# Attention with adapters: turning queries, keys, last tokens and x by transposing DMA instead of on TensorE, with the adapter's steps in a new order

## The chip, the core and the metric

The kernel runs on one core of one Trainium2 chip, in a single launch. The metric is device time in microseconds, as the median over runs. The profile is one more execution, taken by the hardware profiler. The core's engines work side by side, each through its own list of instructions in order: TensorE (PE, with its weight loads shown as PEld), VectorE (DVE), ScalarE (ACT), GpSimd (POOL), and SyncE (SP), which in this kernel only issues DMAs. Engines wait for each other by semaphores.

## The reference

Two stages follow each other: attention with a relative bias, then a mixture of low-rank adapters on the attention's output.

```python
scores = (1 / np.sqrt(D)) * np.matmul(q, k.transpose(0, 1, 3, 2))    # q, k, v: [8, 8, 576, 64]
bias = bias_table[bucket(abs(i - j))]                                # [576, 576, 8 heads], constant from distance 128 on
attn = softmax(scores + bias.transpose(2, 0, 1)[None])
x = np.matmul(attn, v).transpose(0, 2, 1, 3).reshape(4608, 512)

logits = x @ w_gate                                                  # 8 experts
topk = the two largest logits of each row; w = softmax over these two
delta = sum over the two: w * ((x @ A[e]) @ B[e])                    # A: [8, 512, 16], B: [8, 16, 512]
out = x + delta
```

Inputs and output are float32; the kernel computes products in bfloat16 with float32 sums.

## The kernel before

**Units.** The work is cut into 32 units, one for each of 8 batches (`b`) and 4 pairs of heads (`hp`); `u = 4 b + hp`. Of the 576 tokens of a sequence, the first 512 are treated in four key tiles of 128 (`c`), the last 64 ("last tokens", "tail") apart. The whole order is written out by hand: one loop over `u`, in which each engine's instructions stand in the order in which the engine runs them. Nothing is rearranged later.

**Inputs.** SP loads float32 queries, keys and values of a pair into staging tiles (`load`, L99 to L114), queries and keys four units ahead, values three, and the last tokens of a batch once per batch (`load_tail`). GpSimd casts them to bfloat16 (`cast`, L133 to L143; `cast_tail`), queries and keys two units ahead (`prep`). There are four staging buffers of each kind.

**Turns.** A product on TensorE needs the summed dimension on the partitions, so queries and keys, which arrive with tokens on the partitions, must be turned. `Turn.block` (L298 to L303) does it with four TensorE transposes of 64x64 per 128x128 block. They write into a score tile `tp` in PSUM, and VectorE copies the whole to `qkT` in SBUF (`Turn.copy`, L306). Each unit turns the queries and keys of the next unit: eight blocks (`turn_qk`, `copy_qk`); once per batch also the last tokens' (`turn_tail`, `copy_tail`, into `tls`). The score tiles are three PSUM tiles in rotation: four key tiles, the edges and the turn use them in each unit.

**Scores and exponentials.** `keys` (L346 to L361) makes one key tile's scores of two heads, the product with the queries (L353) and a second one that adds the bias (L358); `keys_exp` (L364) takes the exponential on ScalarE, 128x1024 at a time. `edges` (L386 to L402) makes the products of last tokens with the others, with one exponential per unit (`pt`, L402). `edge_bias` multiplies their bias factors on GpSimd and VectorE. The products among last tokens are made once per batch (`turn_corners`, `corners_exp`, `corners_bias`).

**Values.** One unit later the exponentials are multiplied with the values, which carry a column of ones so that the sum of the softmax comes out too. `values_a` covers query tiles 0 to 2, `values_b` tile 3 and the last tokens (L418, L428, L442). Each writes a PSUM bank of 512 float32 columns. `normalise_a` and `normalise_b` divide by the sum and write x in bfloat16 (`xn`, `xe`, L476 to L489) on VectorE. These banks come from a pool of two (`mm`), which also holds the turned x and the adapters' results.

**Adapters.** A batch's x is complete after four units. Its rows form groups: `g0` and `g1` of two tiles of 128 rows each, and a group of last tokens for two batches together. For each group x is turned on TensorE (`turn_x`, L334) and copied by VectorE (`copy_x`, L338); then come the product with A and the gate (`moe_z` in free columns of a values bank, or `moe_zpair` in a bank of its own), the copy out (`moe_zc`), the choice of two experts (`moe_g`, DVE and POOL), the weights (`moe_w`, ScalarE and POOL), the transpose of the gated z (`moe_t`, L559, copied by `moe_tc`, L562), and the product with B with the sum with x (`moe_d`, L566, L569), after which the group is stored by SP. `moe` enters each step into a table for a later unit; the loop takes the tables' entries at fixed places. For the second to last batch (`early`) the steps follow more closely. Steps that would not be done in time go to `left` and are made after the loop (`late_out`), three tiles in all.

**After the loop** the last batch's x is finished, turned (`last_x` and `turn`) and taken through the same adapter steps with code of its own.

**SP's list** in a unit is: last tokens' load (once per batch), queries and keys of `u + 4`, values of `u + 3`, then the stores where `moe_d` stands. SP takes them in this order; a store whose result is not ready holds what stands behind it.

Of the kernel before, what the change touches and what calls it, by code (L numbers as in the profile page):

```python
# [37 lines left out]
def kernel(  # L38
# [94 lines left out]
    def cast(u, nm, eng):  # L133
        s = stage[(u, nm)].rearrange("p h (c d) -> p h c d", c=4)
        if nm == "v":
            t = vts[u % NV]
            eng.tensor_copy(t[:, :, :, :D].rearrange("p c h d -> p h c d"), s)  # L137
        else:
            t = qkp.tile([128, 4, 2, D], BF16, name=f"{nm}n", tag=f"{nm}n")
            copy = eng.copy if eng is nc.scalar else eng.tensor_copy  # L140
            copy(t.rearrange("p c h d -> p h c d"), s)  # L141
            nat[(u, nm)] = t
# [167 lines left out]
    def turn_qk(t, u):  # L310
        for i, nm in enumerate(("q", "k")):
            n = nat.pop((u, nm))
            for c in range(4):
                t.block(4 * i + c, n[:, c, :, :].rearrange("p h d -> p (h d)"))

    def copy_qk(t, u):
        qkT[u] = qkp.tile([128, 2, SM], BF16, name="qkT", tag="qkT")
        t.copy(qkT[u], 0, 8)

# [9 lines left out]
    def turn_x(gr):  # L329
        n = len(gr.x)  # L330
        gr.xT_ps = mp.tile([128, 2, 4, 128], BF16, name="xT_ps", tag="mm")
        for i, x in enumerate(gr.x):
            for c in range(4):
                nc.tensor.transpose(gr.xT_ps[:, i, c, :], x[:, c * 128:(c + 1) * 128], ident)  # L334

    def copy_x(gr):
        gr.xT = xtp.tile([128, len(gr.x), 4, 128], BF16, name="xT", tag="xT")
        nc.vector.tensor_copy(gr.xT, gr.xT_ps[:, :len(gr.x)])  # L338
# [84 lines left out]
    def pv_last(u, pv, o, t, n=1):  # L423
        b, hp = units[u]
        pt = probs[u][1]
        for h in range(2):
            x0 = 64 + h * SM + 256 + t % 2 * 128
            nc.tensor.matmul(_ap(pv, o + h * W1, [[260, n], [1, W1]]), lhsT=pt[:, x0:x0 + 128],  # L428
# [4 lines left out]
    def pv_tail(u, pv, c, o=130, first=False):  # L433
# [10 lines left out]

    def values_a(u):
        pva[u] = mp.tile([128, 512], FP32, name="pv", tag="mm")
        for t in range(3):
            for c in range(4):
                pv_main(u, pva[u], t * 130, t, c, t == 0 and c == 0)
        pv_last(u, pva[u], 0, 0, 2)  # L450
        pv_last(u, pva[u], 130, 1)
        return pva[u]

    def values_b(u):
        pvb[u] = mp.tile([128, 512], FP32, name="pv", tag="mm")
        for c in range(4):
            pv_main(u, pvb[u], 0, 3, c, c == 0)
        pv_last(u, pvb[u], 0, 3)
        for c in range(5):
            pv_tail(u, pvb[u], c)  # L460
# [11 lines left out]

    def normalise_a(u):
# [3 lines left out]
        nc.vector.tensor_tensor(_ap(xs[b], hp * 128, [[Dm, 3], [D, 2], [1, D]]),  # L477
                                _ap(pv, 0, [[2 * W1, 3], [W1, 2], [1, D]]),
                                _ap(rc, 0, [[2, 3], [1, 2], [0, D]]), op=ALU.mult)

    def normalise_b(u):
# [3 lines left out]
        nc.vector.tensor_tensor(_ap(xs[b], 3 * Dm + hp * 128, [[D, 2], [1, D]]),  # L485
                                _ap(pv, 0, [[W1, 2], [1, D]]),
                                _ap(rc, 6, [[1, 2], [0, D]]), op=ALU.mult)
        rows = slice(64 * (b % 2), 64 * (b % 2) + 64)
        nc.vector.tensor_tensor(xe[b // 2][rows, hp * 128:hp * 128 + 128].rearrange("p (h d) -> p h d", h=2),  # L489
                                _ap(pv[rows], 130, [[W1, 2], [1, D]]), _ap(rc[rows], 8, [[1, 2], [0, D]]),  # L490
                                op=ALU.mult)
# [89 lines left out]
    def group(b, i):  # L581
        gr = Group()
        gr.zT_ps, gr.zT, gr.ot, gr.solo = {}, None, None, False
        if i < 2:
            gr.x = [xs[b][:, c, :] for c in (2 * i, 2 * i + 1)]

# [4 lines left out]
        else:  # L591
            gr.x = [xe[b // 2]]

# [5 lines left out]
    late, second, third, tx, zs, zts, ztb, gate1, after = ({} for _ in range(9))  # L599
# [4 lines left out]
    def moe(b, u):  # L604
        g0, g1 = group(b, 0), group(b, 1)
        tiles = ((g0, 0), (g0, 1), (g1, 0), (g1, 1))
        early = b == B - 2
        at(tx, u + 1 - early, g0)
        at(tx, u + 2 - early, g1)
        if early:  # L610
            for i, g in enumerate((g0, g1)):
                at(late, u + i, moe_zpair, g)
                at(gate1, u + 1 + i, moe_w, g)
# [452 lines left out]
```

## Time and profile before

| | us |
|---|---|
| median of 3 runs | 205.93 |
| the three runs | 204.39, 205.93, 206.39 |
| the profiled execution | 205.11 |
| its span | 203.3 |

| engine | busy us in the span | share |
|---|---|---|
| TensorE | 173.8 | 86% |
| ScalarE | 166.1 | 82% |
| VectorE | 138.3 | 68% |
| GpSimd | 130.9 | 64% |
| DMA engines, SP's queue | | 64.7% of 16 engines |

In the rows quoted below, L353 is line 353 of the kernel, `out<-in` names what an instruction writes and reads, `x32` counts instructions, and sizes are partitions x elements. In the groups, the numbers after the first bar are busy us in all and mean ns of one; those after the second bar are idle time of that engine just before these instructions, with what ended most of it. In a timeline a row begins with its start and its length in us, and a bracket at its end gives the idle time before it. SPq is the queue on which SP issues DMAs.

### The profile page before, as it was taken

What the parts mean: (1) busy time and instruction counts of PE and PEld (TensorE: products, weight loads), DVE (VectorE), ACT (ScalarE), POOL (GpSimd) and SP (SyncE); (2) the same over time, 40 slices, a digit from 0 to 9 for tenths busy, and PEclk for the clock granted to TensorE, in tenths of its full rate; (3) what the DMA queues carried; (4) which work ended last, traced back from release to release, by engine and by line L of the source; (5) the groups of instructions that cost most, each with busy time, mean ns of one, the idle gap of its engine ahead of it and who ended that gap; (6) DMA issues with size and microseconds to landing.
All of it is one profiled execution on the core that took longest, in us unless ns stands there. A gap on an engine that the chain in (4) does not pass through costs nothing.

```text
span 203.3 us, 11419 instructions
## 1 busy us (share of the span) xinstructions
PE 173.8 (86%) x4898; PEld 127.5 (63%) x4898; DVE 138.3 (68%) x411; ACT 166.1 (82%) x205; POOL 130.9 (64%) x321
## 2 busy tenths in 40 slices
PE   0377889899999899989988999999988997999870
PEld 0255666677666677766676677767776685666640
DVE  4314655467667876887877777789877786888750
ACT  3269999998998889989879889889988878788470
POOL 4298546678578647986694947985776577761110
PEclk9999999999999999999999999999999999999999
DMA  5868889679778886855279999862498940042165
GB/s 134 214 192 240 235 243 240 177 212 272 213 208 254 252 218 203 242 173 158 58 196 299 280 242 295 251 203 72 108 280 262 291 167 24 3 157 107 55 241 173
DMA packets 62714, 39.87 MB, mean 196 GB/s; under 512 B 17848, under 2 KB 59336, under 8 KB 62664
## 3 DMA queue, kind: packets, MB, share of 16 engines
q1 hardware_dynamic: 61864, 38.58, 64.7%
q8 instruction: 38, 0.62, 1.3%
q10 hardware_dynamic: 800, 0.56, 1.1%
q14 instruction: 12, 0.10, 0.2%
HBM read 29.67 MB, written 9.46 MB: 192 GB/s over the span
## 4 chain that ended last, share of the span: by engine, by line
PE 51%; ACT 18%; DVE 15%; issue 5%; DMA 5%; POOL 2%; ACTq 0%; POOLq 0%; DVEq 0%
PE pv L418 14%; PE sc L353 10%; ACT pk L364 10%; ACT pt L402 6%; PE sc L358 5%; DVE ot L569 5%; PE xT_ps L334 4%; PE pv L428 3%; PE sc L395 3%; PE tp L302 3%; DVE pt L410 2%; PE sc L400 2%; PE dl L566 2%; PE pv L442 2%; DMA Wt<-g_d 1%
## 5 line engine op out<-in xcount | busy, mean ns | idle before, releaser
L364 ACT ACTIVATE pk<-sc 128x1024 bf16<-128x1024 f32 x128 | 124.1, 1028 | 14.6 <-PE sc L358 13.4
L353 PE MATMUL sc<-qkT 64*64 64x512 bf16 x512 | 52.8, 396 | 3.4 <-ACT pk L364 2.7
L418 PEld LDWEIGHTS <-pk 128*128 128x128 bf16 x1024 | 38.7, 98 | 16.4 <-issue 7.8
L358 PE MATMUL sc<-Wt,anti 64*64 64x384 bf16 (+1 forms) x512 | 44.1, 300 | 1.8 <-DMA Wt<-g_d 1.8
L418 PE MATMUL pv<-v,pk 128*128 128x65 bf16 x992 | 42.7, 194 | 0.9 <-DVE z L522 0.4
L402 ACT ACTIVATE pt<-sc 128x1024 bf16<-128x1024 f32 x32 | 32.8, 1024 | 10.3 <-PE sc L400 5.2
L306 DVE COPY qkT<-tp 128x1024 bf16<-128x1024 bf16 x32 | 22.0, 686 | 6.9 <-PE tp L302 6.2
L410 DVE TENSOR_TENSOR pt<-pt,ET 64x256 bf16<-64x256 bf16 x32 | 15.3, 477 | 15.2 <-ACT pt L402 11.9
L353 PEld LDWEIGHTS <-qkT 64*64 64x64 bf16 x512 | 17.1, 106 | 12.7 <-issue 5.7
L137 POOL CAST v<-vs 128x512 bf16<-128x512 f32 x32 | 20.4, 637 | 6.6 <-DMA vs<-in_v_dram 6.5
L141 POOL CAST kn<-ks 128x512 bf16<-128x512 f32 x31 | 19.4, 626 | 1.1 <-PE sc L358 0.9
L358 PEld LDWEIGHTS <-anti 64*64 64x64 bf16 x512 | 17.9, 108 | 2.9 <-issue 2.9
L569 DVE TENSOR_TENSOR ot<-dl,xn 128x512 f32<-128x512 f32 x25 | 17.3, 691 | 1.3 <-PE dl L566 0.3
L477 DVE TENSOR_TENSOR xn<-pv,rc 128x384 bf16<-128x384 f32 x31 | 17.3, 557 | 1.1
L141 POOL CAST qn<-qs 128x512 bf16<-128x512 f32 x27 | 16.6, 613 | 1.6 <-PE sc L358 0.9
L428 PE MATMUL pv<-vb,pt 128*128 128x65 bf16 (+1 forms) x186 | 17.5, 203 | 0.0
L302 PEld LDWEIGHTS <-qn 64*64 64x64 bf16 x512 | 10.8, 111 | 10.4 <-ACT qn L141 5.3
L532 POOL TENSOR_TENSOR a<-z,top 128x16 f32<-128x16 f32 (+1 forms) x17 | 3.8, 223 | 19.2 <-DVE top L527 19.1
L302 PE MATMUL tp<-ident,qn 64*64 64x64 bf16 x512 | 11.1, 196 | 5.7 <-ACT qn L141 5.3
L562 DVE COPY zT<-pv 128x128 bf16<-128x128 bf16 x31 | 6.7, 221 | 12.0 <-PE pv L559 12.0
L408 POOL TENSOR_TENSOR pt<-pt,ELC 128x128 bf16<-128x128 bf16 x32 | 13.8, 431 | 1.5 <-ACT pt L402 1.4
L442 PE MATMUL pv<-v,pt 128*128 128x65 bf16 x248 | 13.0, 193 | 0.0
(147 smaller groups left out, 337.8 us busy)
## 6 DMA issues: line engine op xcount, KB each, us to landing
qs<-in_q_dram SPq DMA_DIRECT2D x32, 256.0 KB, 3.9
vs<-in_v_dram SPq DMA_DIRECT2D x64, 128.0 KB, 4.0
ks<-in_k_dram SPq DMA_DIRECT2D x62, 128.0 KB, 3.8
out_dram<-ot SPq DMA_DIRECT2D x11, 512.0 KB, 4.2
vt<-in_v_dram SPq DMA_DIRECT2D x8, 128.0 KB, 4.1
out_dram<-fot SPq DMA_DIRECT2D x4, 256.0 KB, 2.4
qkt<-in_q_dram SPq DMA_DIRECT2D x7, 128.0 KB, 4.7
qkt<-in_k_dram SPq DMA_DIRECT2D x7, 128.0 KB, 3.9
```

Of the source, the lines that this page charges most:

```text
L137: eng.tensor_copy(t[:, :, :, :D].rearrange("p c h d -> p h c d"), s)
L141: copy(t.rearrange("p c h d -> p h c d"), s)
L302: nc.tensor.transpose(self.ps[h * 64:h * 64 + 64, f, x * 64:x * 64 + 64], src[rows, h * 64:h * 64 + 64], ident[rows, rows])
L306: nc.vector.tensor_copy(_ap(dst, 0, [[64, 2], [128, n], [1, 64]]), self.ps[:, :, x * 64:(x + n) * 64].rearrange("p f (x t) -> p f x t", t=64))
L353: nc.tensor.matmul(sc[prt, h, :], lhsT=kT[rows, c * 128 + f * 64:c * 128 + f * 64 + 64], rhs=qT[rows, :], start=True, stop=False, skip_gro ...
L358: nc.tensor.matmul(_ap(sc[prt, h, :], p0, [[128, 4], [1, n]]), lhsT=turned(h), rhs=_ap(Wt[rows, hp, :], (1 - e) * GY + y0, [[GY, 4], [1, n]]),
L364: nc.scalar.activation(probs[u][0][c], scs.pop(c), ACT.Exp, scale=scale)
L402: nc.scalar.activation(probs[u][1][:, 64:], sc.rearrange("p h x -> p (h x)"), ACT.Exp, scale=scale)
L410: eng.tensor_tensor(te, te, ET[64:, :, hp, :], op=ALU.mult)
L418: nc.tensor.matmul(pv[:, o + h * W1:o + (h + 1) * W1], lhsT=pk[c][:, h, t * 128:(t + 1) * 128], rhs=vm[:, c, h, :], start=(first and h == ...
L428: nc.tensor.matmul(_ap(pv, o + h * W1, [[260, n], [1, W1]]), lhsT=pt[:, x0:x0 + 128], rhs=tvs[b % 2][:, t // 2:t // 2 + n, 2 * hp + h, :], ...
L569: nc.vector.tensor_tensor(gr.ot[:, t, :], dl, gr.x[t], op=ALU.add)
```

## The change

Four parts, cut to their core.

**Queries and keys.** They are cast into one tile instead of two. From the fourth pair on (`DT = 3`), one transposing DMA on SP's queue turns a unit's queries and keys from SBUF to SBUF, issued at the head of the unit before; TensorE's turn and VectorE's copy remain for the first pairs.

```diff
-            t = qkp.tile([128, 4, 2, D], BF16, name=f"{nm}n", tag=f"{nm}n")
+            if u not in nat:
+                nat[u] = qkp.tile([128, 2, 4, 2, D], BF16, name="qkn", tag="qkn")
...
+    def send_qk(u):
+        qkT[u] = qkp.tile([128, 2, SM], BF16, name="qkT", tag="qkT")
+        nc.sync.dma_start_transpose(out=qkT[u].rearrange("p i (c t) -> p (i c) t", c=4),
+                                    in_=nat.pop(u).rearrange("p i c h d -> p (i c h d)"))
+
+    def send_tail(b):
+        nc.sync.dma_start_transpose(out=tls[b % 2], in_=nat[(b, "qk")].rearrange("p h d -> p (h d)"))
...
-    def turn_x(gr):
+    def send_x(gr):
         n = len(gr.x)
-        gr.xT_ps = mp.tile([128, 2, 4, 128], BF16, name="xT_ps", tag="mm")
-        for i, x in enumerate(gr.x):
-            for c in range(4):
-                nc.tensor.transpose(gr.xT_ps[:, i, c, :], x[:, c * 128:(c + 1) * 128], ident)
-
-    def copy_x(gr):
-        gr.xT = xtp.tile([128, len(gr.x), 4, 128], BF16, name="xT", tag="xT")
-        nc.vector.tensor_copy(gr.xT, gr.xT_ps[:, :len(gr.x)])
+        gr.xT = xtp.tile([128, n, 4, 128], BF16, name="xT", tag="xT")
+        nc.sync.dma_start_transpose(out=gr.xT.rearrange("p n c t -> p (n c) t"), in_=gr.flat)
```

**Where the new DMAs stand**, ahead of the unit's loads on SP; the last tokens' load moves from the first unit of the batch before to the last unit of the batch before that:

```diff
-        if hp == 0 and 0 < b < B - 1:
-            load_tail(b + 1)
+        if DT <= u + 1 < NU:
+            send_qk(u + 1)
+        if hp == (2 if b else 3) and b < B - 1:
+            send_tail(b + 1)
+        run(tx.pop(u, []))
+        if hp == 3 and b < B - 2:
+            load_tail(b + 2)
         if u + 4 < NU:
             load(u + 4, "qk")
...
         keys(u, KO[2])
         keys_exp(u, KO[2])
-        if u < NU - 1:
+        if u + 1 < DT:
             t = Turn()
             turn_qk(t, u + 1)
-            if hp == 0:
-                cps = mp.tile([128, 256], FP32, name="cps", tag="mm")
-                turn_corners(cps, b)
-            if hp == HP - 1:
-                turn_tail(t, b + 1)
             copy_qk(t, u + 1)
```

From the fifth unit on, the cast of the values (`prep_v`) stands after the unit's first two key tiles, not at its head with the other casts.

**The values** are shared out anew: `values_a` takes query tiles 0 and 2 and the last tokens, `values_b` tiles 1 and 3; the normalising steps go with them.

```diff
     def values_a(u):
-        for t in range(3):
+        for t in (0, 2):
             for c in range(4):
-                pv_main(u, pva[u], t * 130, t, c, t == 0 and c == 0)
+                pv_main(u, pva[u], t * W1, t, c, t == 0 and c == 0)
         pv_last(u, pva[u], 0, 0, 2)
-        pv_last(u, pva[u], 130, 1)
+        for c in range(5):
+            pv_tail(u, pva[u], c, 260)
...
     def values_b(u):
-        for c in range(4):
-            pv_main(u, pvb[u], 0, 3, c, c == 0)
-        pv_last(u, pvb[u], 0, 3)
-        for c in range(5):
-            pv_tail(u, pvb[u], c)
+        for t in (1, 3):
+            for c in range(4):
+                pv_main(u, pvb[u], (t - 1) * W1, t, c, t == 1 and c == 0)
+        pv_last(u, pvb[u], 0, 1, 2)
```

**The adapters' steps.** The transpose of z and the product with B come one unit later than before, the special order of the second to last batch goes, and four tiles instead of three are left for after the loop; two of their transposes of z come there too.

```diff
         if b == B - 2:
             g0.solo = g1.solo = True
+            at(late, u + 1, moe_zpair, g0)
+            at(gate2, u + 2, moe_w, g0)
+            at(mid, u + 2, moe_zpair, g1)
+            at(gate1, u + 3, moe_w, g1)
+            for i in range(2):
+                at(ztb, u + 3, *tiles[i])
+            at(second, u + 2, moe_d, *tiles[0])
+            left.extend(tiles[1:])
...
-                at(zts, u + 4 + i, g, t)
-                if b < B - 3 or i < 3:
-                    at(second, u + 4 + i, moe_d, g, t)
...
+                    at(zts, u + 5 + i, g, t)
+                if o and i == 2:
+                    left.append((g, t))
+                else:
+                    at(second, u + 5 + i - 2 * (o and i == 3), moe_d, g, t)
```

In the loop, `second` (the product with B) moves from after the first two key tiles to just before `values_a`; `late` and `third` and `last_x`, which stood at the unit's end, move to its middle, one unit later. `moe_zc` and `moe_tc` now always follow `normalise_b`.

147 lines of the change are left out of this document (66 added, 81 removed).

## The prediction

> **What bounds the kernel now.** I read the page first (span, chain), then stretches, then ScalarE's timeline, then one unit of the pipeline, then the DMA queue. The profiled execution took 205.11 us, of which 203.3 are its span; the median of the runs shown is 205.93 (204.39 to 206.39), 0.8 above it. All sums below are differences against the profiled execution, and the forecast puts them on the median.
>
> ```profile
> span 203.3 us, 11419 instructions
> ...
> PE 51%; ACT 18%; DVE 15%; issue 5%; DMA 5%; POOL 2%; ACTq 0%; POOLq 0%; DVEq 0%
> ```
>
> The chain of waits runs mostly through TensorE. The next row is one stretch, from the pipeline's third unit to its last (columns: length, then busy us and count of PE, PEld, DVE, ACT, POOL, then granted clock, DMA share, GB/s).
>
> ```profile
> 28.31:182.76 154.45, 144.15 (x4187) 107.24 (x4179) 116.39 (x338) 136.68 (x165) 112.31 (x267) 1.00 0.69 201
> ```
>
> TensorE is busy 144.15 of 154.45 us at full clock, ScalarE 136.68. So even if TensorE's load fell far, ScalarE's idle 17.8 us is all that this stretch can give. How much of that is really to be had is seen in ScalarE's timeline, where the row `pt<-sc` comes once per head pair and so marks the units:
>
> ```profile
> 28.31 1.02 ACT L402 ACTIVATE pt<-sc 128x1024 bf16<-128x1024 f32 x1 [0.31 <-issue]
> 29.23 3.77 ACT L364 ACTIVATE pk<-sc 128x1024 bf16<-128x1024 f32 x4
> 33.30 1.02 ACT L402 ACTIVATE pt<-sc 128x1024 bf16<-128x1024 f32 x1 [0.31 <-issue]
> ...
> 49.30 1.02 ACT L402 ACTIVATE pt<-sc 128x1024 bf16<-128x1024 f32 x1
> ...
> 163.75 1.02 ACT L402 ACTIVATE pt<-sc 128x1024 bf16<-128x1024 f32 x1 [0.34 <-POOL a L534]
> ...
> 182.76 1.02 ACT L402 ACTIVATE pt<-sc 128x1024 bf16<-128x1024 f32 x1
> ```
>
> Before the adapters run, a unit takes 33.30 - 28.31 = 4.99 us: 0.92 (29.23 - 28.31) + 3.77 of exponentials and 0.31 idle. That is ScalarE's pace. From 49.30 to 163.75 lie 21 units of 5.45 us, and from there to 182.76 three of 6.34. With adapters, TensorE is what is late.
>
> **The change part by part. Turns off TensorE.** One unit in detail (all engines' timeline, TensorE rows):
>
> ```profile
> 154.94 0.61 PE L334 MATMUL xT_ps<-ident,xn 128*128 128x128 bf16 x8 [0.73 <-DVE ot L569]
> ...
> 155.82 0.32 PE L302 MATMUL tp<-ident,qn 64*64 64x64 bf16 x14
> ...
> 155.98 0.32 PE L302 MATMUL tp<-ident,kn 64*64 64x64 bf16 x14
> ...
> 156.12 0.42 PE L353 MATMUL sc<-qkT 64*64 64x512 bf16 x4
> ...
> 157.73 0.30 PE L395 MATMUL sc<-qkT,tl 64*64 64x256 bf16 x4
> ...
> 163.22 0.30 PE L395 MATMUL sc<-qkT,tl 64*64 64x256 bf16 x4
> ```
>
> The query/key turn holds TensorE from 155.82 to 156.30, 0.48 us per unit; it goes in 29 of the 32 units. A turn of x costs 0.61 us, 14 times, with 0.73 us of waiting in front of it here for a PSUM bank that VectorE still reads. VectorE loses the copies behind both:
>
> ```profile
> L306 DVE COPY qkT<-tp 128x1024 bf16<-128x1024 bf16 x32 | 22.0, 686 | 6.9 <-PE tp L302 6.2
> ...
> L338 DVE COPY xT<-xT_ps 128x1024 bf16<-128x1024 bf16 (+1 forms) x17 | 10.7, 630 | 1.0 <-PE xT_ps L334 1.0
> ...
> L334 PE MATMUL xT_ps<-ident,xn 128*128 128x128 bf16 x112 | 8.5, 218 | 5.1 <-DVE ot L569 4.4 <-ACT pcx L376 0.7
> ```
>
> That is 29 x 0.686 + 10.7 = 30.6 us of VectorE, and on TensorE 29 x 0.48 = 13.9 us, 8.5 of x turns and the 5.1 of idle time ahead of them: 27.5 us, about 1 us per unit. One of six tiles per unit also leaves the three score banks of PSUM, so key tiles stop queueing behind a copy. TensorE per unit falls from 5.45 to about 4.5, below ScalarE's 4.99. ScalarE takes over: I set 5.1 (4.99 plus the small gate and corner activations). The gain is 21 x (5.45 - 5.1) = 7.35 us. The last three units keep their pile of adapter steps; I give them a gain of 1.6 (half of what 5.3 us a unit would give).
>
> **Other layouts of the values** cost nothing: the products are the same but for two last-token matmuls fewer per unit, and the two normalising steps move 256 + 128 columns and 256 in place of 384 and 128 + 128.
>
> **The end.** Four outputs are left for after the last unit, not three, and two more transposes of gated z.
>
> ```profile
> L566 PE MATMUL dl<-Bc,zT 128*128 128x512 bf16 x28 | 10.9, 390 | 0.1
> ...
> L562 DVE COPY zT<-pv 128x128 bf16<-128x128 bf16 x31 | 6.7, 221 | 12.0 <-PE pv L559 12.0
> ...
> L949 ACT COPY lo<-f 128x512 f32<-128x512 f32 x3 | 1.8, 587 | 0.6 <-PE f L939 0.5
> ```
>
> A further 0.39 + 0.59 plus one 0.22 copy that nothing hides is +1.2 us, at most; if they fit in idle time, 0. I take 1.2.
>
> **What SP must now do.** The trace has no transposing DMA, so its price is bounded by the rows of plain ones (durations in ns, minimum/median/maximum):
>
> ```profile
> L113 SPq DMA_DIRECT2D qs<-in_q_dram x32: 380/420/1758, 1.2 to 157.8; - x32
> ...
> DMA to landing us min/median/max: 3.1/3.9/5.6
> ```
> ```profile
> L110 SPq DMA_DIRECT2D ks<-in_k_dram x62: 367/463/1717, 3.7 to 159.2; - x62
> ```
> ```profile
> L110 SPq DMA_DIRECT2D vs<-in_v_dram x64: 378/460/1612, 4.8 to 162.1; - x64
> ```
> ```profile
> L589 SPq DMA_DIRECT2D out_dram<-ot x14: 333/366/1437, 67.3 to 187.7; - x14
> L578 SPq DMA_DIRECT2D out_dram<-ot x6: 513/567/1429, 98.9 to 179.0; - x6
> ```
> ```profile
> L129 SPq DMA_DIRECT2D qkt<-in_q_dram x9: 607/622/1464, 1.6 to 143.7; - x9
> L129 SPq DMA_DIRECT2D qkt<-in_k_dram x9: 613/634/1974, 2.4 to 144.4; - x9
> ```
> ```profile
> L123 SPq DMA_DIRECT2D vt<-in_v_dram x8: 596/634/1487, 7.8 to 145.7; - x8
> ```
>
> By medians these are 96 us: 3.0 per unit. A q load moves 256 rows of 1 KB in 0.42 us of SP, a tail load 512 rows of 256 bytes in 0.62. A turn of 128x1024 is 1,024 rows of 256 bytes; along that slope I estimate 1.0 us, and 0.62 for 128x512. From below it is 0.33 (an issue cannot cost less than the shortest row), from above 1.76 if it is held up like the slowest q load. There are 53: 29 for pairs, 14 for x, 3 for last-token x, 7 for last-token queries and keys, that is 43 large and 10 small, 49 us or 1.5 per unit. SP stands at 4.55 us of a 5.1 us unit: just enough.
>
> **The new waits.** A pair's turn waits on SP until the keys of the pair before last have been read (two buffers), until the casts are done, and behind a store that waits for VectorE; an x turn waits for the last normalising step. Queued behind are the loads, which have two units of room, over 10 us against landings of 5.6 at most, so they hold. In the unit quoted, the last read of qkT ends at 156.54 and the next unit's edges start at 163.22: 6.7 us, 6.3 at the new pace, in which the turn must be issued and land. A plain load lands in 3.9 (median) to 5.6. It fits, with 0.7 to spare at the worst; but a store or two x turns ahead of it eat that. For such units I charge 2 us in all (about ten of them, 0.2 each); the bounds are 0 and what a landing rival below says.
>
> **The DMA engines.** Rows of 256 bytes are what the last-token loads move; they were what moved in the first and the last stretch below, wide rows in the two between:
>
> ```profile
> 101.00:102.00 1.00, 0.80 (x25) 0.54 (x18) 0.97 (x3) 1.00 (x3) 0.84 (x3) 1.00 0.64 144
> ...
> 107.00:108.00 1.00, 1.00 (x34) 0.89 (x27) 0.67 (x2) 1.00 (x2) 0.25 (x2) 1.00 1.15 388
> ...
> 115.00:116.00 1.00, 1.00 (x30) 0.76 (x23) 0.48 (x2) 1.00 (x2) 1.00 (x3) 1.00 1.11 399
> ```
> ```profile
> 145.00:146.00 1.00, 0.90 (x27) 0.91 (x28) 0.81 (x3) 1.00 (x3) 0.92 (x3) 1.00 0.59 133
> ```
>
> At full share that is 144 / 0.64 = 225 GB/s and 133 / 0.59 = 225 against 388 / 1.15 = 337 and 399 / 1.11 = 359. The turns carry 43 x 256 KB + 10 x 128 KB = 12.6 MB, 0.45 MB a unit: 2.0 us at 225, 1.25 at 359. Present traffic is 0.69 x 154.45 / 28 = 3.8 us a unit. The sum is 5.05 to 5.8; I take 291 GB/s (201 / 0.69, the mean of the long stretch, as the turns touch no HBM): 5.35. That is above 5.1, but the share passes 1 where packets overlap, so I do not let it set the pace. The Trainium skill (Advanced Engine Details and Errata, X-Bar Transpose (TRN2)) says that transposing DMAs run as fast as plain ones, 350 to 400 GB/s. By that the turns would take 1.2 us a unit and the DMA engines would never bind; no row here shows a transposing one.
>
> **The sum:** -7.35 - 1.6 + 1.2 + 2.0 = -5.75 us: 199.4 for the profiled execution, 200.2 on the median.
>
> **Rivals. DMA engines bind (slower).** If a turn's packets run at the 225 GB/s of the 256-byte rows, a unit is 5.8 us, so 28 x 5.8 = 162.4 in place of 154.45, with the 1.2 at the end +9.2: 215. For it: the share of 0.69 as a mean over the long stretch with peaks at 1.15, and one queue, so that turns stand behind loads. Against it: SP leaves the queue idle today,
>
> ```profile
> SPq L578 <- DVE ot L569: 12.6, 2, 6.5
> ```
>
> 6.5 us at a time behind one store. It decides from 0.45 MB / (5.5 - 3.8) us = 265 GB/s downward.
>
> **Landing takes TensorE's place (no change).** If turns land 0.5 us later than the room allows in every unit, the unit is 5.5 again: 207 with the longer end. The slowest landing row, 5.6, with 0.4 of store issue and 0.5 of queue ahead, would do it.
>
> **SP binds (slower).** If the hardware takes a turn as eight blocks, each with an issue of its own at 0.42, one costs 3.4 us, SP stands at 3.0 + (43 x 3.4 + 10 x 1.7) / 32 = 8.1 us a unit, and 28 x 8.1 = 227 in place of 154: about 279. It decides from 1.7 us per turn on. The Trainium skill (VectorE: DVE Perf Modes, The three transpose paths) speaks for it: 1,309 ns for one 128x128 block by DMA against 390 on TensorE; eight in a row would be 10.5 us, beyond a unit. Against its TensorE figure stands the row above, eight blocks in 0.61 us.
>
> **How the numbers follow.** Forecast 0.44 (its own range 195 to 203.5: no exposed landings and a free end below, 0.2 us more per unit above); better than that, 0.04 (ScalarE's idle 0.31 goes as well); no change 0.19; DMA binds 0.23; SP binds 0.10. A measurement of this kernel tells about 1% from no change. So faster 0.48, same 0.19, slower 0.33. The range 195 to 218 leaves out the better case, SP's case and 0.04 of the DMA case's upper end.
>
> **What would show it.** Right: no `tp` and `xT_ps` rows after the third unit, ScalarE's `pt<-sc` rows 5.0 to 5.2 us apart from 49 us on, idle time ahead of the edges' matmuls not put down to a DMA, turns on SP near 1 us. Wrong: edges or adapter products waiting for `qkT` or `xT` by DMA, the DMA share above 0.95 over long stretches, or turn issues above 1.7 us with SP never idle.

## The result, and the profile after

| | before | after |
|---|---|---|
| median, us | 206.16 (204.39 to 206.82) | 250.44 (246.98 to 251.54) |
| ratio | | 1.208 (1.201 to 1.216) |
| profiled execution, span | 205.11, 203.3 | 251.54, 249.6 |

The change makes the kernel 21% slower; the forecast was 200.2, in a range of 195 to 218. The profiled execution of after is the slowest of its four runs, 1.8% above the fastest, and the ratio leaves it out. These are the page's rows that answer to those of before: span, granted clock in 40 slices, the DMA queue (packets, MB, share of 16 engines), the chain by engine, and two groups.

```profile
span 249.6 us, 8950 instructions
...
PEclk9999959889979889995897959889795897999997
...
q1 hardware_dynamic: 112712, 51.17, 91.5%
...
PE 27%; DMA 24%; SPq 5%; POOL 5%; DVE 4%; issue 3%; ACT 3%; POOLq 0%; DVEq 0%; ACTq 0%
...
L404 ACT ACTIVATE pt<-sc 128x1024 bf16<-128x1024 f32 x32 | 32.8, 1026 | 57.6 <-PE sc L402 37.6
...
L397 PE MATMUL sc<-qkT,tl 64*64 64x256 bf16 x128 | 11.0, 319 | 53.0 <-DMA qkT<-qkn 48.8
```

TensorE's share of the chain fell from 51% to 27%, and DMA's rose from 5% to 24%. The edges' matmuls, first to read a unit's turned tile, wait 48.8 us for it. ScalarE then waits for the edges.

**Where the 46.3 us of span lie.** ScalarE's timeline of after, one row per unit, at the start and the end of the stretch that the prediction used, with two pairs in it:

```profile
32.80 1.02 ACT L404 ACTIVATE pt<-sc 128x1024 bf16<-128x1024 f32 x1 [3.50 <-issue]
...
60.86 1.02 ACT L404 ACTIVATE pt<-sc 128x1024 bf16<-128x1024 f32 x1 [2.37 <-issue]
65.39 1.07 ACT L404 ACTIVATE pt<-sc 128x1024 bf16<-128x1024 f32 x1
...
135.43 1.02 ACT L404 ACTIVATE pt<-sc 128x1024 bf16<-128x1024 f32 x1 [0.17 <-POOL qkn L142]
146.10 1.02 ACT L404 ACTIVATE pt<-sc 128x1024 bf16<-128x1024 f32 x1 [5.89 <-PE sc L402]
...
228.21 1.02 ACT L404 ACTIVATE pt<-sc 128x1024 bf16<-128x1024 f32 x1 [0.95 <-PE sc L402]
```

The stretch of 28 units is 228.21 - 32.80 = 195.4 us, against 154.45 before: +41.0. Its start is 4.5 later, and what follows it takes 0.9 more. A unit takes 6.98 us instead of 5.52. A unit at ScalarE's pace exists (65.39 - 60.86 = 4.53), beside one of 10.67 (146.10 - 135.43). The same stretch by engines (columns as in the prediction):

```profile
32.80:228.21 195.41, 143.42 (x3001) 102.15 (x2997) 81.44 (x279) 136.11 (x163) 109.79 (x259) 0.87 1.01 215
```

ScalarE and GpSimd do what they did; VectorE's 116.39 fell to 81.44. TensorE has 1,186 matmuls fewer, yet is busy as long as before, at a mean granted clock of 0.87. What fills up is DMA, and the list that issues it. SP's timeline of after (start, length, instruction):

```profile
129.96 1.33 SPq L322 DMA_TRANSPOSE qkT<-qkn  x1
131.41 2.72 SPq L340 DMA_TRANSPOSE xT<-xn  x2
134.18 2.02 SPq L113 DMA_DIRECT2D qs<-in_q_dram  x1
136.57 0.88 SPq L110 DMA_DIRECT2D ks<-in_k_dram  x2
137.50 1.02 SPq L110 DMA_DIRECT2D vs<-in_v_dram  x2
138.62 0.41 SPq L595 DMA_DIRECT2D out_dram<-ot  x1
139.13 1.80 SPq L322 DMA_TRANSPOSE qkT<-qkn  x1
141.03 1.96 SPq L326 DMA_TRANSPOSE tl<-qkb  x1
```

SP's rows never carry a bracket; its waits show as gaps between the end of one row and the start of the next. Here no gap is longer than 0.4 us: one issue follows the other. The turn issued at 139.13 is the one for which the unit at 146.10 waits; the chain of waits has its landing:

```profile
139.13 6.23 DMA qkT<-qkn
```

**SP's sum.** Adding the lengths of SP's timeline rows over the stretch gives 106.2 us before and 178.5 after. Gaps under 0.2 us between issues add 8.5 and 10.1; longer waits, 37.9 before, are 3.8 after. So SP was idle for a quarter of the stretch, and is now idle for 2% of it. The DMA engines are full as well: their share of the stretch rose from 0.69 to 1.01. Either can make the loads and turns late, and the runs below have to part them.

### The profile page after: what moved, and what is told of

Read it like the earlier page. It is cut to its first block, busy times and chain, and to the rows that moved or that the text cites. A ratio compares the mean times of both kernels' runs of the same rounds, so it can differ in the third digit from the quotient of the medians.

```text
span 249.6 us, 8950 instructions
## 1 busy us (share of the span) xinstructions
PE 173.3 (69%) x3675; PEld 123.1 (49%) x3676; DVE 103.9 (42%) x357; ACT 166.1 (67%) x206; POOL 130.6 (52%) x321
## 2 busy tenths in 40 slices
DMA packets 113552, 52.29 MB, mean 209 GB/s; under 512 B 68696, under 2 KB 110184, under 8 KB 113512
## 3 DMA queue, kind: packets, MB, share of 16 engines
q1 hardware_dynamic: 112712, 51.17, 91.5%
## 4 chain that ended last, share of the span: by engine, by line
PE 27%; DMA 24%; SPq 5%; POOL 5%; DVE 4%; issue 3%; ACT 3%; POOLq 0%; DVEq 0%; ACTq 0%
DMA qkT<-qkn 21%; PE pv L420 7%; PE sc L355 6%; PE sc L360 4%; DMA xT<-xn 2%; PE sc L397 2%; SPq L110 2%; PE pv L504 2%; PE pv L430 1%; PE dl L571 1%; SPq L340 1%; PE pv L444 1%; SPq L113 1%; POOL qkn L142 1%; DMA vs<-in_v_dram 1%
## 5 line engine op out<-in xcount | busy, mean ns | idle before, releaser
L355 PE MATMUL sc<-qkT 64*64 64x512 bf16 x512 | 61.7, 450 | 0.8 <-ACT pk L366 0.6
L360 PE MATMUL sc<-Wt,anti 64*64 64x384 bf16 (+1 forms) x512 | 51.2, 343 | 2.9 <-DMA Wt<-g_d 2.9
L397 PE MATMUL sc<-qkT,tl 64*64 64x256 bf16 x128 | 11.0, 319 | 53.0 <-DMA qkT<-qkn 48.8
L412 DVE TENSOR_TENSOR pt<-pt,ET 64x256 bf16<-64x256 bf16 x32 | 10.5, 329 | 69.8 <-ACT pt L404 66.5
L142 POOL CAST qkn<-qs 128x512 bf16<-128x512 f32 x27 | 16.4, 609 | 25.1 <-DMA qkT<-qkn 14.5
L478 DVE TENSOR_TENSOR xn<-pv,rc 128x256 bf16<-128x256 f32 x62 | 26.3, 425 | 2.1
L142 POOL CAST qkn<-ks 128x512 bf16<-128x512 f32 x31 | 19.3, 621 | 0.0
L430 PE MATMUL pv<-vb,pt 128*128 128x130 bf16 x124 | 18.8, 237 | 0.0
L495 DVE RECIPROCAL rc<-pv 128x4 f32<-128x4 f32 x31 | 5.7, 183 | 18.3 <-PE pv L504 12.6
L384 POOL TENSOR_TENSOR pc<-pcx,ELC 64x256 bf16<-64x256 bf16 x16 | 10.6, 664 | 4.1 <-ACT ELC L233 2.0
```

The source lines that it names most:

```text
L142: copy(nat[u][:, "qk".index(nm)].rearrange("p c h d -> p h c d"), s)
L355: nc.tensor.matmul(sc[prt, h, :], lhsT=kT[rows, c * 128 + f * 64:c * 128 + f * 64 + 64], rhs=qT[rows, :], start=True, stop=False, skip_gro ...
L360: nc.tensor.matmul(_ap(sc[prt, h, :], p0, [[128, 4], [1, n]]), lhsT=turned(h), rhs=_ap(Wt[rows, hp, :], (1 - e) * GY + y0, [[GY, 4], [1, n]]),
L397: nc.tensor.matmul(sc[prt, h, 256:], lhsT=tl[rows, 64:], rhs=qT[rows, f * 256:f * 256 + 256], start=True, stop=True, skip_group_check=True)
L430: nc.tensor.matmul(_ap(pv, o + h * W1, [[130, n], [1, W1]]), lhsT=pt[:, x0:x0 + 128], rhs=tvs[b % 2][:, t // 2:t // 2 + n, 2 * hp + h, :], ...
L478: nc.vector.tensor_tensor(_ap(xs[b], t * Dm + hp * 128, [[2 * Dm, 2], [D, 2], [1, D]]), _ap(pv, 0, [[2 * W1, 2], [W1, 2], [1, D]]), _ap(rc ...
```

## The experiments

The question was what makes a turn late: the transposing as such, the bytes on the DMA engines, the landing time, the new order, or SP's list. Kernels that ran once (all but the first two) stand beside runs of the kernel before on the same chip, 204.6 to 206.5 in every set. "SP sum" below is the sum of SP's timeline rows over the whole span: 142.3 for the kernel before, 213.5 for the changed one. A row that stands for several issues holds the gaps between them too, some of them waits; the issues alone add up to 131.5 and 209.0.

**New order, all turns on TensorE** (`DT = NU`, and the turns of x and of last tokens as TensorE transposes in the middle of the unit):

```diff
-    DT = 3
+    DT = NU
-        if hp == (2 if b else 3) and b < B - 1:
-            send_tail(b + 1)
-        run(tx.pop(u, []))
...
+            if xg:
+                turn_x(xg[0])
...
+            if hp == HP - 1:
+                turn_tail(t, b + 1)
```

> All turns back on TensorE and VectorE; what is left of the change is the new order of the adapter's steps and the new split of the values. If the order itself costs much, this stays above 225 us. If the transposing DMAs are the cause (by whichever of the three ways below), it comes out between 203 and 209 us, the longer end of the list being the only cost.

205.37 us (203.59 to 208.22) against 206.48: ratio 0.993 (0.988 to 0.998). The order, the other value layouts and the longer end cost nothing together; the kernel is about as fast as before. All of the 21% comes with the transposing DMAs.

**Pairs alone back on TensorE** (`DT = NU`; x and last tokens stay on DMA):

> Queries and keys of all pairs are turned on TensorE; the 24 turns of x and of last tokens stay transposing DMAs. Theory SP (a turn holds SP's list for 1.2 us or more, and the list sets the pace): SP falls from 214 us of work by 29 x 1.6 = 47 to 167, so 203 to 210 us. Theory engines (the turns' packets fill the 16 DMA engines): 24 of 53 turns and 5.0 of 12.6 MB stay, so some 0.4 of the loss stays, 215 to 225 us. Theory lead (a pair's turn lands later than the one unit it has): the turns left have more than a unit of room, 198 to 206 us.

220.57, ratio 1.068 (1.058 to 1.077). The 24 turns that remain cost 15 us over the run above, and SP's sum goes from 136.9 to 171.8. That is the range expected if the DMA engines set the pace; for the list alone 203 to 210 were expected.

**x alone back on TensorE** (`turn_x` and `copy_x` as before, pairs and last tokens on DMA):

> The 17 turns of x go back to TensorE, the 36 of pairs and last tokens stay on SP. Theory SP (each turn holds SP's list for 1.2 us or more whatever its size): SP is rid of 25 us and no unit has three turns in a row any more; 222 to 235 us. Theory lead (a pair's turn is issued too late for the one unit it has, however full SP is): the pairs' turns are as late as before in most units, so above 235 us.

237.06: without the 17 turns of x, 13 us of the 45 are gone. The turns of x cost too, though the edges don't read them. The time is 2 us above the range expected for the list, and so in the one expected if a pair's turn comes too late in any case; the runs with earlier turns below speak against that.

**One block per turn** (seven eighths of each large turn, and three quarters of each of last tokens, are left out; those parts are zeros):

```diff
-        nc.sync.dma_start_transpose(out=gr.xT.rearrange("p n c t -> p (n c) t"), in_=gr.flat)
+        nc.sync.dma_start_transpose(out=gr.xT.rearrange("p n c t -> p (n c) t")[:, :1], in_=gr.flat[:, :128])
```

> Every transposing DMA is still issued in its place, but turns only its first 128x128 block; the other blocks of the turned tiles stay zero, so the scores and the adapter's products are computed on other data. Theory SP: the issue costs the same for 128x512 and 128x1024 (1.22 us at least), so it stays here too; 53 issues of 1.2 and the loads make 160 to 200 us of SP, and the time stays above 220 us. Theory engines: the turns' packets fall to about one seventh, the time falls to 196 to 208 us. Theory lead: a block lands sooner than eight; between 200 and 215 us, with waits for qkT gone.

245.09: only 5 us less. SP's row for the pairs' turns (ns, minimum/median/maximum) and the queue's share in this kernel:

```profile
L327 SPq DMA_TRANSPOSE qks<-qkn x29: 1093/1262/2287, 30.0 to 214.0; - x29
```
```profile
q1 hardware_dynamic: 70344, 40.33, 60.3%
```

and the same row of the changed kernel:

```profile
L322 SPq DMA_TRANSPOSE qkT<-qkn x29: 1231/1367/3092, 28.1 to 220.7; - x29
```

The DMA engines are back below the share of before (64.7%), the issue is hardly shorter, and the time stays. So with most of the bytes gone something else holds the kernel at 245: SP's list, or the transposing as such.

**Plain copies of the same bytes** (nothing is turned: the tiles hold their source's layout):

```diff
-        nc.sync.dma_start_transpose(out=qkT[u].rearrange(...), in_=...)
+        nc.sync.dma_start(out=qkT[u].rearrange(...), in_=...)
```

> Each transposing DMA is replaced by a plain copy of the same bytes from the same tile into the same tile, in 256-byte rows, in the same place of SP's list; nothing is turned, so scores and adapter's products are computed on other data. Theory SP: a plain issue of this many rows costs 0.4 to 1.0 us, SP falls by 30 to 60 us, 200 to 220 us. Theory engines, if it is the bytes: 12.6 MB at the 225 GB/s of 256-byte rows take 56 us in place of the 97 us that the turns took, so 225 to 235 us. Theory engines, if it is the transposing that is slow: 200 to 210 us.

217.93. The row for the pairs:

```profile
L322 SPq DMA_DIRECT2D qkT<-qkn x29: 470/514/1888, 28.8 to 187.2; - x29
```

An issue costs 0.51 instead of 1.37 us, and 33 of the 45 us are gone. The packets came out as wide rows (18,696 of them under 512 bytes against 68,696 in the changed kernel), so price of issue and size of packets fall together here; the later runs part them. The 12 us that stay are to be noted: even at half the price that the prediction took for a turn, the change would have lost.

**Values' loads issued by GpSimd** (`load(u + 3, "v", nc.gpsimd)`):

> In the loop the loads of values are issued from GpSimd's queue instead of SP's; nothing else changes. Theory SP: its list loses the 36 us of these loads, a seventh of its work, and the time falls to 215 to 228 us. Theory engines or lead: the same bytes and the same turns in the same places, the time stays above 240 us.

249.4. SP's sum falls only to 199.5: turns and loads are held longer (54 us of `qkT` issues against 47). The list alone would have given 215 to 228. It is not the only limit: SP's queue takes 84.6% of the DMA engines' span and GpSimd's 14.8%, so the engines have no room left. GpSimd, now 171 us busy, issues and casts too, so the run does not tell more.

**Turns issued a unit earlier** (three buffers in place of two, casts three units ahead):

```diff
-        if DT <= u + 1 < NU:
-            send_qk(u + 1)
+        for w in (u + 1,) if u < 4 else (5, 6) if u == 4 else (u + 2,):
+            if DT <= w < NU:
+                send_qk(w)
```

> A pair's queries and keys are cast and turned one unit earlier (two units ahead of their use from the seventh pair on, with three buffers for the cast and for the turned tile); SP's list has the same entries. Theory lead: the waits for qkT go, 205 to 220 us. Theory SP: the list is as long as before, so the unit is as long too, 238 to 250 us, and the waits only change their place.

255.31, above the 238 to 250 expected for the list and far above the 205 to 220 for late turns. The edges no longer wait for turns (6.4 us in all), but the casts now wait for the loads:

```profile
POOL qkn L142 <- DMA qs<-in_q_dram: 50.0, 18, 4.9
```

The 48.8 us moved to another place: an early turn is a late load. **Both together:**

> Both of the edits before: turns two units ahead, and the loads of values on GpSimd's queue. Theory SP: as with the loads alone, 215 to 228 us, since the list's length decides; if lead and list both count, this is the one that comes near or below the kernel before, 198 to 212 us.

241.31, with an SP sum of 195.6, above both ranges expected. The DMA engines are full again (87.7% and 13.3% for the two queues).

**More room everywhere** (five staging buffers, loads one unit earlier, x turns ahead of the pair's), on top of the earlier turns:

> Turns two units ahead of their use as in the run before (7 ahead), and now the loads and casts one unit earlier too, with five staging buffers, and the turns of x ahead of the pair's turn on SP. Every DMA has at least one unit more than in the changed kernel. If late landings are the cause, 203 to 215 us. If throughput is (SP's list or the DMA engines), 235 us or more.

257.26. With more lead for each transfer the time does not fall at all. That is no question of landing time, but of throughput, of SP's list or of the DMA engines.

**The same with values' loads on GpSimd,** and **the same with one block per turn as well** (leaving out what the block run above leaves out):

> As the run before, with the loads of values on GpSimd's queue from the fifth unit on, so that SP's list is a seventh shorter. If SP's list is the limit once the leads are long, 15 to 25 us below the run before; if the DMA engines are, within 5 us of it.

> As the run before (leads and values on GpSimd's queue), but each transposing DMA turns only its first 128x128 block, the other blocks of the turned tiles stay zero. If the 256-byte packets of the turns fill the DMA engines, 200 to 212 us, well below the run before; if what costs is one transposing DMA as such, whatever it carries (its issue, or a stall of the queue around it), within 6 us of the run before.

236.99 and 225.54. The first is within the range expected for the list, but its DMA engines are full (87.6% and 10.4%). The second is between the two ranges expected: with blocks the time falls by 11 us, so the packets cost too, but not down to 212. GpSimd is busy 165.7 us in it, 90% or more in half of the slices: here GpSimd may limit too.

**The DMAs alone** (only transfers in groups of twelve, with no attention; zeros are stored as the output):

> Nothing of the computation: zeros are stored, then DMAs run by themselves on SP's queue, 12 of a kind, each kind after the one before has landed: turns of 128x1024, turns of 128x128, plain copies of 128x1024, q loads of 256 KB, turn and load in turns, copy and load in turns. If a turn's issue of 1.2 us is its own cost, it shows here with an empty queue, for one block as for eight. If its packets are slow, twelve whole turns take more than 12 x 1.3 us to land (above 2 us each), blocks do not. If a turn stalls the plain traffic beside it, turn and load in turns take longer than the two kinds by themselves added up (turns about 1.3 to 2 us each, loads about 0.9).

SP's rows for turns of 128x1024 (`tw`), for turns of one block, and for turns of 128x1024 alternating with query loads:

```profile
L84 SPq DMA_TRANSPOSE tw<-src x12: 1327/1337/11959, 12.8 to 40.3; - x12
```
```profile
L87 SPq DMA_TRANSPOSE tb<-src x12: 1132/1230/1232, 46.5 to 60.4; - x12
```
```profile
L84 SPq DMA_TRANSPOSE tm<-src x12: 1237/1237/1266, 90.6 to 111.9; - x12
```

and the stretches of whole turns, of blocks, and of turns with loads (DVE, POOL, clock, DMA share, GB/s):

```profile
28.00:42.00 14.00, 0.00 (x0) 0.00 (x0) 1.00 1.01 192
46.48:62.00 15.52, 0.00 (x0) 0.00 (x0) 1.00 0.12 25
90.64:114.00 23.36, 0.00 (x0) 0.00 (x0) 1.00 1.07 245
```

A block costs SP 1.23 us with DMA at 0.12, so there this price alone sets the pace; a whole turn between loads costs 1.24. Whole turns in a row run at 192 GB/s with the DMA engines full: 256 KB take 1.37 us of them, and the issue lasts 1.34. The first of them, issued while the stores of zeros were still landing (up to 16.0 us after their issue), held SP for 11.96 us. So an issue's row can hold time in which the transfers ahead of it are still moving. A turn and a load, alternating, take 1.93 us for the pair, no more than by themselves (1.38 and 0.56 from issue to issue): here a turn does not stall the plain traffic beside it.

**Keys and values by one load per pair** (two issues of SP fewer in a unit; keys and values have another order of tokens in their tiles):

```diff
-                for h in range(2):
-                    eng.dma_start(out=t[:, h, :].rearrange("p (g x) -> p g x", g=2), ...)
+            eng.dma_start(out=t, in_=heads.rearrange("h (p c) d -> p h (c d)", c=4))
```

> The changed kernel with keys and values of a pair loaded by one DMA each, as queries are, in place of one per head; SP loses some 62 issues of 0.5 us, 32 us, and no other engine gets them. Keys and values then stand in another token order, so the scores are computed with the bias of other positions. If SP's list is the limit, 212 to 225 us; if the lead of one unit is, above 235 us.

235.91. Two cheap issues less in a unit give back 14.5 us, with the same turns and bytes (the loads' rows are longer: 96,143 packets in place of 113,552). The time stays above the 212 to 225 expected if the list were the only limit. The queue's row shows what holds it now:

```profile
q1 hardware_dynamic: 95576, 51.17, 98.6%
```

SP has room again (its sum is 191.6 of 234.0), the DMA engines have none. **With more room as well:**

> The run before with the longer leads of the slack run (257 us): turns, casts and loads one unit earlier. If list and lead both count, 203 to 215 us; if the list alone does, the same as the run before within 5 us; if the DMA engines do, above 225 us.

234.63, with the DMA engines at 99.7%: again nothing from room.

**Turns that nobody reads.** The kernel of the first run, with TensorE's turns, issues the 53 transposing DMAs in addition, into spare tiles:

```diff
+    def spare_qk(u):
+        t = qkp.tile([128, 2, SM], BF16, name="sqk", tag="sqk")
+        nc.sync.dma_start_transpose(out=t.rearrange("p i (c t) -> p (i c) t", c=4),
+                                    in_=nat[u].rearrange("p i c h d -> p (i c h d)"))
...
+        if 3 <= u + 1 < NU:
+            spare_qk(u + 1)
```

> All turns that count are made on TensorE (as in the first run of the new order alone, 205.4 us); besides, every transposing DMA of the changed kernel is issued in its place on SP, with its waits for casts and x, into spare tiles that nothing reads. If the cost is in engines that wait for a landed turn, it is gone: 204 to 210 us. If SP's list or the DMA engines are the cause, loads and stores come late whoever reads the turns: 222 to 245 us.

262.16 (205.37 without them). It is above the 222 to 245 expected for the list or the DMA engines. No product waits for a turn, and yet the kernel is slower than the changed one. One consumer is left, as a cast may not overwrite a source that a spare turn has still to read. **With blocks only:**

> As the run before, each spare turn with its first 128x128 block only. If the issues on SP are the cost, within 5 us of the run before; if the packets are, half of the way back to 205 us or more.

248.75, with the queue at 59.1%: 13 us less, neither within 5 us nor half of the way back. Both the issues and the packets cost, the issues more.

**Blocks with the short list of loads** (leaving out what the block run leaves out, in the token order of the one-load run):

> The merged loads (236 us), with turns of one 128x128 block only; the other blocks stay zero, keys and values stand in another token order. If, once SP's list is shorter, the turns' packets on the DMA engines are the next limit, 205 to 222 us; if it is still the list, 228 to 236 us, as one block costs SP as much as eight.

219.68, against 235.91 with whole turns. With the shorter list, the size of the turns matters: 16 us, as expected if the DMA engines are the next limit.

**Three tiny plain copies in place of each spare turn** (16 rows of 256 bytes each; no transposing DMA is left):

```diff
-        nc.sync.dma_start_transpose(out=t.rearrange("p i (c t) -> p (i c) t", c=4), in_=...)
+        for i in range(3):
+            nc.sync.dma_start(out=t[16 * i:16 * i + 16, 0, :128], in_=...[16 * i:16 * i + 16, :128])
```

> As the spare blocks (249 us), with every transposing DMA into a spare tile replaced by three tiny plain copies (16 rows of 256 bytes each) in the same place, with the same waits for casts and x, to take about the same 1.2 us of SP. Nothing is transposed by DMA, and next to no bytes move. If it is the time on SP's list that costs, 230 to 250 us; if it is something of the transposing DMA itself, 204 to 215 us.

277.17. The pairs' copies on SP, and the share of DMA in 40 slices of this kernel:

```profile
L342 SPq DMA_DIRECT2D sqk<-qkn x87: 507/587/1858, 27.6 to 250.2; - x87
```
```profile
DMA  5788636443560448433664426635467164613436
```

Without any transposing, with almost no bytes more than the kernel on TensorE and with the DMA engines about half idle, this is the slowest kernel of all. It is above the 230 to 250 expected because three copies held SP for 2.1 us and not for 1.2: the rows of the 159 issues add up to 112 us of SP's list, those of the 53 turns to 83. So time on SP's list is enough by itself. Its waits show how a late issue reaches the rest: the casts wait for the copies of their old source.

```profile
POOL qkn L142 <- DMA sqk<-qkn: 67.0, 16, 7.6
```

**All runs against SP's list and the DMA engines** (us; the span, what is left of it beside SP's sum, and the share of the DMA engines' span that SP's and GpSimd's queues took):

| kernel | SP sum | span | rest | DMA, % |
|---|---|---|---|---|
| all on TensorE | 136.9 | 204.3 | 67.4 | 64.9 |
| before | 142.3 | 203.3 | 61.0 | 64.7 |
| x and last tokens by DMA | 171.8 | 217.6 | 45.8 | 83.1 |
| plain copies | 174.0 | 216.1 | 42.1 | 76.7 |
| one load, blocks | 175.5 | 217.6 | 42.1 | 64.3 |
| room, GpSimd, blocks | 181.6 | 223.8 | 42.2 | 70.2 |
| x on TensorE | 190.2 | 235.3 | 45.1 | 86.5 |
| one load | 191.6 | 234.0 | 42.4 | 98.6 |
| one load, room | 192.7 | 232.8 | 40.1 | 99.7 |
| earlier and GpSimd | 195.6 | 239.5 | 43.9 | 101.0 |
| values' loads by GpSimd | 199.5 | 247.6 | 48.1 | 99.4 |
| room, GpSimd | 199.7 | 235.2 | 35.5 | 98.0 |
| blocks | 206.8 | 242.9 | 36.1 | 60.3 |
| after | 213.5 | 249.6 | 36.1 | 91.5 |
| spare blocks | 216.2 | 246.8 | 30.6 | 59.1 |
| turns earlier | 217.7 | 253.5 | 35.8 | 93.7 |
| more room | 218.0 | 255.5 | 37.5 | 89.2 |
| spare turns | 228.2 | 260.2 | 32.0 | 95.0 |
| spare tiny copies | 247.5 | 275.4 | 27.9 | 48.6 |

From 137 to 142 us SP's sum makes no difference; from 172 on the span grows with it, and the rest, 28 to 48 us, is the small gaps (about 12), the list's start and the waits that its order still has. The sum is not a price list alone: it holds also issues that last 2 to 3 us where their median is 0.4 to 1.4, and these grow with the traffic (the one-load run loses 16 us of SP's sum when its turns shrink to blocks). The last column shows the other limit. Five kernels with a shorter list have the DMA engines at 98% or more and stay at 235 to 249 us; those with blocks have the engines free, and a long list keeps them at 245 to 249. Only where both are relieved does the time come to 226 or less. In the changed kernel both are full.

## Why the prediction was wrong, step by step

**What bounds the kernel: right as far as seen; the relief of TensorE did not show.** A unit of 4.53 us (above) shows that ScalarE's pace is within reach without the turns, as the 5.1 assumed. It is reached in few units, since the tile is not there. VectorE lost 34.95 us in the stretch, where 30.6 were expected. TensorE's busy time did not fall, as the same work ran at a lower clock: `sc<-qkT` takes 450 ns each here and 394 in the all-TensorE kernel.

**The values' layouts: right,** at nothing. **The end:** +1.2 expected, +0.9 measured behind the last `pt`.

**"What SP must now do": the step that failed first,** in both of its terms.
- *The present load.* "By medians these are 96 us: 3.0 per unit" left out what medians hide. SP's rows add up to 142.3 us; in the stretch to 106.2, that is 3.8 per unit, and 4.1 with the gaps between issues. The slow rows of the quoted groups (1.4 to 2.0 us as maximum) are not rare: 8 of the 62 issues of keys last over 1 us, and all 62 add up to 38.5 us, not 62 x 0.463 = 28.7. In the trace of before this stood open to be read, in SP's timeline:

```profile
114.51 0.38 SPq L113 DMA_DIRECT2D qs<-in_q_dram  x1
114.99 1.37 SPq L110 DMA_DIRECT2D ks<-in_k_dram  x2
116.45 0.93 SPq L110 DMA_DIRECT2D vs<-in_v_dram  x2
117.43 0.62 SPq L129 DMA_DIRECT2D qkt<-in_q_dram  x1
118.10 1.15 SPq L129 DMA_DIRECT2D qkt<-in_k_dram  x1
119.29 0.63 SPq L123 DMA_DIRECT2D vt<-in_v_dram  x1
120.02 0.57 SPq L113 DMA_DIRECT2D qs<-in_q_dram  x1
```

  SP fills a whole unit without a long wait here, between its long waits for stores. That it was working off what those waits had held up is likely, but no run shows it.
- *The price of a turn.* 1.0 us (0.62 for the small) came from a slope by rows. Measured alone it is 1.23 for a block and 1.24 to 1.34 for a whole turn; in the kernel the 53 sum to 82.4 us, 1.55 each, in place of 49. This lies within the bounds given (0.33 to 1.76), but on the far side of the price that decides (worked out below). Together: 52 of the turns, 81.0 us, lie in the stretch, and 4.1 + 81.0 / 28 = 7.0, less 0.1 for stores (their issues in it fell from 10.4 to 7.9 us), against 6.98 us per unit measured; the prediction had 4.55.

**"SP stands at 4.55 us of a 5.1 us unit: just enough" is also wrong as a rule.** The plain copies, at 0.51 us, leave SP waits of 24.9 us in the span and still take 218. Their DMA engines stand at 76.7%. A list in fixed order seems to need room for what holds it.

**The new waits.** "Two units of room ... so they hold" assumed that SP comes to a load in time. With SP full, loads, turns and stores all are late, and moving one ahead makes another late (turns earlier: 48.8 us of waits for turns became 50.0 for loads). The charge of 2 us stood for landings; landing was not what set the time, as the runs with more room show. The turns land in 4.7 us by median (3.2 to 6.2), inside the 6.3 that the prediction found.

**"The DMA engines": the second step that failed.** The prediction had 3.8 us a unit for the present traffic and 1.55 for the turns, 5.35 in all, and did not let it set the pace. In the stretch the share is now 1.01, which makes 1.01 x 6.98 = 7.05 a unit: the turns added 3.2, twice the term. Alone, a turn's bytes run at 192 GB/s, below the lower bound of 225 that came from rows of 256 bytes; the time of packets in the full kernel is longer still. So the DMA engines' time, too, stood above the 5.1 of a unit. The two limits lie close together: with an eighth of the bytes the time is 245, and with the short list alone 236; only both together give 220. The Trainium skill (Advanced Engine Details and Errata, X-Bar Transpose (TRN2)) has transposing DMAs as fast as plain ones, at 350 to 400 GB/s. The runs disagree: 192 for whole turns.

**The rivals.** SP binding, at 0.10, and the DMA engines binding, at 0.23, were the right mechanisms, each at the wrong price. For SP the prediction took eight issues of 0.42 per turn, 3.4 us, and gave 279; it is one issue of 1.24. Its "decides from 1.7 us per turn on" was worked out from the 3.0 per unit. From 4.1, with 52 turns in the 28 units of the stretch, it is (5.52 - 4.1) / 1.86 = 0.76 us, which the turn exceeds. The Trainium skill's 1,309 ns for a block (VectorE: DVE Perf Modes, The three transpose paths) is near the issue's price, but it does not add up by blocks: eight cost SP about what one costs, and land 4.7 us after the issue begins, against 3.4 in the block run. The DMA rival took 225 GB/s and gave 215; with SP relieved, the DMA engines alone hold the kernel at 235 or more. The landing rival's 207 would have needed room on both.

**Open.** Why some issues on SP last 2 to 3 us is not shown. They come with busy DMA engines, and the DMAs alone show one issue held for 11.96 us behind stores; but they come in the tiny-copies run too. So how much of SP's sum is the price of issues, and how much the engines' doing, is not settled for the changed kernel. The runs with GpSimd's queue do not tell what a second free queue would give, since GpSimd was full of casts and the DMA engines were full. The 45 us do not divide into a part for the list and a part for the engines, as each hides behind the other: 14.5 came back when two loads per unit left the list, 5 when most of the turns' bytes went, and 31 with both.

## What to carry to other kernels

Before moving work to a DMA, add up the issuing engine's timeline, all its rows and gaps rather than medians times counts, stage by stage, as one would for TensorE; in these runs an in-order list that was full made the transfers late, and buffers or earlier places only chose which. Add up the DMA engines' time in the same way, with the transfers that are to come. Here the price of a transposing issue hardly depended on its size, so fewer and larger ones should relieve such a list; the one-load run shows it for loads, larger turns were not tried. When a wait names a DMA, look first at when it was issued, and only then at how fast it ran.

## What the runs showed of the hardware

Alone, a transposing DMA from SBUF to SBUF holds SP for 1.23 us at 32 KB and for 1.24 to 1.34 at 256 KB, where a plain copy of 256 KB holds it for 0.6 (`cw<-src`, median 605 ns).

Idle stretches cost TensorE more than their length. In the changed kernel (columns as in the prediction's windows):

```profile
139.00:140.00 1.00, 0.40 (x12) 0.25 (x8) 0.65 (x4) 1.00 (x2) 0.92 (x3) 1.00 0.91 269
...
142.00:143.00 1.00, 0.00 (x0) 0.00 (x0) 0.00 (x0) 0.00 (x0) 0.00 (x0) 1.00 2.46 112
143.00:144.00 1.00, 0.00 (x0) 0.00 (x0) 0.00 (x0) 0.00 (x0) 0.00 (x0) 0.95 0.15 28
144.00:145.00 1.00, 0.00 (x0) 0.00 (x0) 0.00 (x0) 0.00 (x0) 0.00 (x0) 0.50 0.94 208
...
149.00:150.00 1.00, 1.00 (x13) 0.66 (x16) 0.82 (x3) 0.00 (x0) 0.00 (x0) 0.50 1.24 237
```

The last matmul ends at 139.4. Some 4.5 us later, shortly before 144, the granted clock falls to 0.50, and it is still there in the slice from 149 on, though matmuls run again from 145.4 on. The Trainium skill (TensorE: Matmul & The Clock Gate, Part 1) states this fall after an idle window of about 3.4 us; the trace agrees, as the idle time was longer than that. The row from 142 on also shows a DMA share of 2.46 at 112 GB/s, followed by 0.15 at 28: the packets that began in that microsecond took long, and few began in the next. What held them is open.
